# Attention with Fourier mixing on one core: storing every head pair's divided sums in 64-row transfers

## The chip, the core and the metric

The kernel runs on one core of a Trainium2 chip. The metric is the device time of one execution in microseconds (us). The kernel before takes 1719.1 us, the median of three runs (1718.28 to 1724.07). Its profiled execution took 1721.98 us.

## What is computed

The inputs are x (2048 rows, 512 columns), weights for an attention layer and matrices of a discrete Fourier transform. Cut to what matters:

```python
g = sigmoid((x * gate_w).sum(-1, keepdims=True))
q, k, v = split(x @ wqkv)                        # 32 heads of 16 columns
p = softmax(einsum("hqd,hkd->hqk", q, k) * 16 ** -0.5)
a = merge(einsum("hqk,hkd->hqd", p, v)) @ wo
b = dft_seq_re @ (x @ dft_hid_re.T) - dft_seq_im @ (x @ dft_hid_im.T)
return g * a + (1 - g) * b
```

## The kernel before

The program is one instruction stream per engine: TensorE (PE) multiplies, VectorE (DVE) and ScalarE (ACT) work on its results, GpSimd (POOL) does elementwise work and issues some transfers, and SyncE (SP) issues most of the others. The order on each engine is written out by hand: a schedule of steps, with loads, splits and stores placed at fixed step numbers.

Until about 665 us the kernel projects queries, keys and values, forms the first Fourier products, and scans many score blocks for row maxima, which the softmax needs before its exponentials. Then comes the main loop (L1197). It takes the 32 heads as 16 pairs, each pair as two halves of 1024 queries, and each half as 16 steps, one per block of 128 keys: 512 steps. The diff touches what is done with the result of each half, of which there are 32; the last is finished in another way behind the loop, so 31 go through the lines below.

One step does the following on PE: scores of a key block against 1024 queries (`qk`, L229), a scan block for a later pair's maxima (L154), and the sums of probabilities times values (`pv`, L775), which accumulate in one PSUM tile `pvb` over the 16 steps of a half. ACT forms the exponentials (L253, L261). DVE reduces each scan block to its maxima (L156); PE may not write the next scan block into that PSUM tile before DVE has read the last one. From step 317 on (MIX, at about 1268 us) the scans are over, and Fourier and output products (L204) take their place on PE.

`va`, the values, has a column of ones per head. So `pvb` holds, for each of four quarters (two heads and two blocks of 512 queries, at rows 0, 32, 64 and 96), 16 rows of sums and in a 17th row the softmax's denominators. When a half is complete:

- `quotients` (L782): DVE copies `pvb` into `ob` (L784). POOL issues four small transfers (L787) that spread the four rows of denominators over 128 partitions in `lc`.
- Ten steps later (L1240 to L1244), `divide` (L791): DVE takes the reciprocal of `lc` (L793). This instruction stands in DVE's stream among the reductions L156, so that one that waits here keeps the reductions behind it waiting. POOL then stores `lc` to DRAM (L794), loads it back as four broadcasts into `rb` (L796), multiplies (L797), rounds the product to `oh` (L808), takes the remainder `ol` (L811), and stores both to `o_d` (L803, or L806 for the last pair, which goes through SP's queue).

POOL issues its transfers in the order of its stream, and they travel on one queue, the profile's q0 (software_dynamic). SP's transfers are on q1 (hardware_dynamic). The next half's denominators (L787) come next on POOL's queue behind a half's two stores.

`o_d[f][i]` is a DRAM tile of shape 2, 2, 4, 64, 512: half, block of queries, pair within its group of four, 64 rows, 512 columns. One store of `oh` therefore writes two blocks of 64 rows by 2 KB that lie apart in DRAM, from 128 partitions in SBUF. These stores are read again only from 1562 us on, by SP's loads (L859, L867, L879, L882) for the output projection.

Of the kernel before, what the change touches and what calls it, by code (L numbers as in the profile page):

```python
# [10 lines left out]
F32 = mybir.dt.float32  # L11
# [12 lines left out]
NP = H // 2  # L24
# [42 lines left out]
def build(tc, xT, wqkv, wo, wrT, wiT, cr, ci, ct, gate, out):  # L67
    nc = tc.nc
    with ExitStack() as ctx:
# [18 lines left out]
        o_d = [[dram.tile([2, 2, NP // ND, 64, 512], F32, name=f"o_d{f}_{i}") for i in range(2)] for f in range(ND)]  # L88
# [181 lines left out]
        with ExitStack() as pf:  # L270
# [381 lines left out]
            with ExitStack() as py:  # L652
# [36 lines left out]
                for n, (ph, t, u) in enumerate(coef):  # L689
# [34 lines left out]
                    for w in range(CS):  # L724
                        s = u * CS + w
# [24 lines left out]
        with ExitStack() as pa:  # L750
# [40 lines left out]
            def divide(p, h, ob, lc):  # L791

                nc.vector.reciprocal(lc, lc)  # L793
                nc.gpsimd.dma_start(r_d[p][h].rearrange("n (s e) -> (n s) e", e=16), lc)  # L794
                for n, (c, j, r) in enumerate(quads):
                    nc.gpsimd.dma_start(rb[r:r + DH, :], r_d[p][h][n:n + 1, :].to_broadcast([DH, 512]))  # L796
                nc.gpsimd.tensor_mul(ob, ob, rb)  # L797
                oh, ol = (ap.tile([P, 512], F32R, tag=tag, name=tag) for tag in ("oh", "ol"))
                queue = nc.sync if p == NP - 1 else nc.gpsimd

                def store(i, s):
                    if p < NP - 1:
                        queue.dma_start(o_d[p // 4][i][h, :, p % 4], s.bitcast(F32))  # L803
                        return
                    for c in range(2):
                        queue.dma_start(o_d[p // 4][i][h, c, p % 4], s[64 * c:64 * c + 64, :].bitcast(F32))  # L806

                nc.gpsimd.tensor_copy(oh, ob)  # L808
                if p == NP - 1:
                    store(0, oh)  # L810
                nc.gpsimd.tensor_sub(ol, ob, oh.bitcast(F32))  # L811
                if p < NP - 1:
                    store(0, oh)
                store(1, ol)
# [382 lines left out]
            for step in range(NP * PERIODS):  # L1197
                p, i = step // PERIODS, step % PERIODS
                h, kb = i // NB, i % NB
# [132 lines left out]
```

## Time and profile before

| what | us |
|---|---|
| median of three runs | 1719.1 |
| profiled execution, its own time | 1721.98 |
| its span, from the first to the last instruction | 1720.2 |
| PE busy in the span | 1703.2 |
| ACT busy in the span | 1497.3 |
| DVE busy in the span | 1190.2 |
| POOL busy in the span | 752.1 |

How to read the profile: one execution, times in us from the span's start. A row of a view that groups instructions gives line, engine, operation, tiles (out<-in), shapes and count. A row of the timeline gives the start, the duration, and in brackets how long the engine had sat idle and what ended that. The view of waits gives who waited for whom: total, number of times, longest. The chain of waits is followed back from the last instruction. For a transfer issued by POOL the trace also has the time to landing; for one of SP it has not. The small difference between the execution's time and its span, 1.8 us, lies outside the instructions.

### The profile page before, as it was taken

What the parts mean: (1) busy time and instruction counts of PE and PEld (TensorE: products, weight loads), DVE (VectorE), ACT (ScalarE), POOL (GpSimd) and SP (SyncE); (2) the same over time, 40 slices, a digit from 0 to 9 for tenths busy, and PEclk for the clock granted to TensorE, in tenths of its full rate; (3) what the DMA queues carried; (4) which work ended last, traced back from release to release, by engine and by line L of the source; (5) the groups of instructions that cost most, each with busy time, mean ns of one, the idle gap of its engine ahead of it and who ended that gap; (6) DMA issues with size and microseconds to landing.
All of it is one profiled execution on the core that took longest, in us unless ns stands there. A gap on an engine that the chain in (4) does not pass through costs nothing.

```text
span 1720.2 us, 36368 instructions
## 1 busy us (share of the span) xinstructions
PE 1703.2 (99%) x13560; PEld 1029.4 (60%) x13560; DVE 1190.2 (69%) x2179; ACT 1497.3 (87%) x2472; POOL 752.1 (44%) x849
## 2 busy tenths in 40 slices
PE   9999999999999999999999999999999999999998
PEld 6888888989888795333333333333345555555554
DVE  6898888899999996666566666666742555654343
ACT  6447889888888888999899999999998888898876
POOL 3672435755555761434534445353422333334222
PEclk9999999999999999999999999999999999999999
DMA  7783457543337764456545545544445466676733
GB/s 254 242 287 77 149 160 215 161 112 107 107 112 199 181 127 95 93 116 157 109 111 140 121 114 114 120 112 97 76 93 135 130 150 146 148 150 167 194 104 126
DMA packets 174881, 241.17 MB, mean 140 GB/s; under 512 B 75968, under 2 KB 86704, under 8 KB 168112
## 3 DMA queue, kind: packets, MB, share of 16 engines
q1 hardware_dynamic: 133520, 217.27, 47.9%
q0 software_dynamic: 40608, 20.54, 6.1%
q8 instruction: 106, 1.74, 0.4%
q10 hardware_dynamic: 576, 1.05, 0.2%
q14 instruction: 71, 0.58, 0.1%
HBM read 158.34 MB, written 81.01 MB: 139 GB/s over the span
## 4 chain that ended last, share of the span: by engine, by line
PE 92%; DMA 4%; POOL 1%; DVE 1%; issue 1%; SPq 0%; ACT 0%; DVEq 0%; POOLq 0%
PE xy L204 26%; PE pvb L775 26%; PE s L229 17%; PE s L173 9%; PE s L204 9%; PE s L154 5%; DMA lc<-ob 2%; DMA rb<-r_d 1%; DMA r_d<-lc 1%; DMA raws<-wqkv 0%; POOL o_d L803 0%; POOL rb L796 0%; POOL lc L787 0%; POOL ob L797 0%; POOL ol L811 0%
## 5 line engine op out<-in xcount | busy, mean ns | idle before, releaser
L253 ACT ACTIVATE eb<-s 128x1024 f32<-128x1024 f32 x512 | 577.2, 1127 | 62.7 <-PE s L229 62.5
L261 ACT ACTIVATE e<-s 128x512 f32<-128x512 f32 x1022 | 606.5, 703 | 4.1 <-PE s L229 4.1
L156 DVE TENSOR_REDUCE mx<-s 128x2 f32<-128x1024 f32 x380 | 460.7, 1223 | 197.6 <-PE s L154 197.4
L775 PE MATMUL pvb<-eb,va 128*17 128x512 f32 x2052 | 516.1, 599 | 0.0
L775 PE MATMUL pvb<-e,va 128*17 128x512 f32 x2044 | 515.2, 599 | 0.0
L179 DVE CUSTOM_DVE_ANT_0 fold<-s,fold 128x512 f32<-128x512 f32 x644 | 433.5, 690 | 56.3 <-PE s L173 29.8
L177 ACT ACTIVATE fold<-s 128x512 f32<-128x512 f32 x644 | 381.6, 603 | 76.6 <-PE s L173 55.7
L229 PEld LDWEIGHTS s<-qs,ks 50*128 50x128 f32 x2048 | 212.9, 185 | 363.4 <-ACT eb L253 266.2
L229 PE MATMUL s<-qs,ks 50*128 50x512 f32 x2048 | 424.1, 436 | 0.0
L204 PE MATMUL xy<-b,c 64*128 64x512 f32 x2448 | 392.8, 392 | 0.3 <-ACT c L352 0.3
L173 PE MATMUL s<-ks,qs 48*128 48x512 f32 x1288 | 304.1, 403 | 1.3 <-DVE mx L179 0.9
L204 PEld LDWEIGHTS xy<-b,c 64*128 64x128 f32 x2448 | 282.8, 187 | 18.9 <-issue 1.0
L173 PEld LDWEIGHTS s<-ks,qs 48*128 48x128 f32 x1288 | 165.6, 184 | 40.6 <-DVE mx L179 10.2
L775 PEld LDWEIGHTS pvb<-eb,va 128*17 128x17 f32 x2052 | 69.8, 96 | 190.5 <-issue 181.2
L154 PE MATMUL s<-ks,qs 48*128 48x512 f32 x760 | 158.6, 396 | 4.8 <-DVE mx L156 4.6
L204 PE MATMUL s<-b,b 64*128 64x512 f32 x1050 | 136.7, 391 | 0.0
L794 POOL DMA_DIRECT2D r_d<-lc x31 | 18.3, 591 | 223.5 <-DVE lc L793 197.2
L204 PE MATMUL xy<-w,b 64*128 64x512 f32 x768 | 114.9, 392 | 0.0
L204 PEld LDWEIGHTS s<-b,b 64*128 64x128 f32 x1050 | 100.2, 185 | 23.8 <-issue 1.0
L384 POOL TENSOR_TENSOR c<-craw,c 128x512 fp32r<-128x512 f32 x84 | 110.4, 1314 | 6.7
L787 POOL DMA_DIRECT2D lc<-ob x124 | 64.4, 526 | 110.9 <-DVE ob L784 110.7
L967 POOL TENSOR_TENSOR sum<-craw 128x512 f32<-128x512 f32 x60 | 75.5, 1286 | 79.0 <-DMA kept_None<-sum 57.6
(148 smaller groups left out, 1538.9 us busy)
## 6 DMA issues: line engine op xcount, KB each, us to landing
qs<-q_d SPq DMA_DIRECT2D x68, 256.0 KB
craw<-cr SPq DMA_DIRECT2D x60, 256.0 KB
craw<-ct SPq DMA_DIRECT2D x48, 256.0 KB
ks<-k_d SPq DMA_DIRECT2D x46, 256.0 KB
kept_None<-sum SPq DMA_DIRECT2D x40, 256.0 KB
craw<-kept_None SPq DMA_DIRECT2D x40, 256.0 KB
qs<-q_d SPq DMA_DIRECT2D x68, 128.0 KB
craw<-ci SPq DMA_DIRECT2D x32, 256.0 KB
```

The source lines that it names most:

```text
L154: nc.tensor.matmul(ps[:, j, :], qs[b:b + 48, qb * P:(qb + 1) * P], ks[b:b + 48, c * 512:(c + 1) * 512], start=True, stop=True)
L156: nc.vector.tensor_reduce(mx[p][:, :, qb, c], ps, axis=AX.X, op=ALU.max)
L173: nc.tensor.matmul(ps, qs[b:b + 48, qb * P:(qb + 1) * P], ks[b:b + 48, c * 512:(c + 1) * 512], start=True, stop=True)
L177: nc.scalar.activation(fold[j], ps, AF.Relu)
L179: nc.vector.tensor_tensor_reduce(out=fold[j], in0=ps, in1=fold[j], scale=1.0, scalar=-3.0e38, op0=ALU.add, op1=ALU.max, accum_out=mx[p][:, ...
L204: nc.tensor.matmul(ps[j], lhs[r], rhs[r], start=first, stop=last)
L229: nc.tensor.matmul(pss[j], ks[b:b + 50, kb * P:(kb + 1) * P], qs[b:b + 50, q0:q0 + 512], start=True, stop=True)
L253: nc.scalar.activation(e, ps, AF.Exp, scale=SCALE)
L261: nc.scalar.activation(e[j], pss[j], AF.Exp, scale=SCALE)
L384: sub(lo, raw, hi.bitcast(F32))
L775: nc.tensor.matmul(pvb[r:r + VC, :], va[:, kb, 2 * p + j, :], es[c][j], start=kb == 0, stop=kb == NB - 1, tile_position=(0, r))
L967: (nc.gpsimd.tensor_add if terms[1][1] > 0 else nc.gpsimd.tensor_sub)(s, *(raws[k] for k, sign in terms))
```

## The change

For the pairs 0 to 14, the store of `oh` and that of `ol` become two transfers each, of 64 rows by 512 columns, in place of one that names two blocks of 64 rows. The last pair's stores have had this form already. The queue is as before: POOL's for the pairs 0 to 14, SP's for pair 15. The stores go to the same places and hold the same values. On POOL a half thus issues 13 transfers in place of 11; no other engine's instructions change, nor their order. Lines behind L801 move up by three.

```diff
@@ -799,9 +799,6 @@
                 queue = nc.sync if p == NP - 1 else nc.gpsimd
 
                 def store(i, s):
-                    if p < NP - 1:
-                        queue.dma_start(o_d[p // 4][i][h, :, p % 4], s.bitcast(F32))
-                        return
                     for c in range(2):
                         queue.dma_start(o_d[p // 4][i][h, c, p % 4], s[64 * c:64 * c + 64, :].bitcast(F32))
```

## The prediction

> **What bounds the kernel now.** The page comes first: which engine is full, and how much room the one that issues the changed transfers has.
>
> ```profile
> span 1720.2 us, 36368 instructions
> ...
> PE 1703.2 (99%) x13560; PEld 1029.4 (60%) x13560; DVE 1190.2 (69%) x2179; ACT 1497.3 (87%) x2472; POOL 752.1 (44%) x849
> ```
>
> PE is busy 99% of the span, so only what lets PE wait or slows it can count; POOL, at 44%, has slack on average. Where does PE lose anything in the main loop? The view of waits says that, first by PE alone, then for the engine that PE waited for.
>
> ```profile
> PE s L154 <- DVE mx L156: 4.6, 2, 3.4
> ...
> DVE lc L793 <- DMA lc<-ob: 8.4, 4, 4.3
> ```
>
> PE waits 4.6 us for DVE's reductions, in two places, and DVE in turn waits 8.4 us, four times, for the denominators' transfer `lc`. The chain of waits, cut to a window around the longest, tells what came before:
>
> ```profile
> 806.77 13.39 DMA rb<-r_d
> ...
> 823.62 1.65 POOL o_d L803 x2
> ...
> 826.79 9.12 DMA lc<-ob
> 836.04 0.25 DVE lc L793
> 836.29 1.09 DVE mx L156
> 837.42 0.79 PE s L154 x2
> ```
>
> Read it upwards. PE's scan block of 837.42 waited for a reduction, that one for the reciprocal, that one for `lc`, which landed 9.12 us after its issue, right behind two stores of `o_d` on POOL's queue. POOL was late because `rb` had taken 13.39 us. The store's own cost to PE is thus one of waiting, and the timeline of PE shows its size. These are scan blocks, one per step:
>
> ```profile
> 831.98 0.40 PE L154 MATMUL s<-ks,qs 48*128 48x512 f32 x2
> ...
> 837.42 0.79 PE L154 MATMUL s<-ks,qs 48*128 48x512 f32 x2 [3.39 <-DVE mx L156]
> ...
> 841.00 0.63 PE L154 MATMUL s<-ks,qs 48*128 48x512 f32 x2
> ...
> 844.31 0.40 PE L154 MATMUL s<-ks,qs 48*128 48x512 f32 x2
> ...
> 846.20 0.40 PE L154 MATMUL s<-ks,qs 48*128 48x512 f32 x2
> ```
>
> An undisturbed step takes 846.20 - 844.31 = 1.89 us. From 831.98 to 844.31 there are three, which took 12.33 in place of 5.67: **6.66 us lost**. Of that 3.39 is idle time. The rest is slowness: the same pair of matmuls takes 0.79 and 0.63 us before it is back at 0.40. The table by stage shows it in the granted clock (the number ahead of the last two):
>
> ```profile
> 700.00:800.00 100.00, 100.00 (x740) 38.15 (x734) 67.75 (x63) 100.00 (x160) 40.89 (x53) 1.00 0.49 113
> 800.00:900.00 100.00, 96.61 (x694) 35.84 (x695) 63.75 (x61) 93.90 (x149) 39.35 (x52) 0.97 0.59 122
> ```
>
> The stage with the stall has a mean clock of 0.97, its neighbour 1.00. Two more places lose time:
>
> ```profile
> 959.79 0.39 PE L154 MATMUL s<-ks,qs 48*128 48x512 f32 x2
> ...
> 963.95 0.40 PE L154 MATMUL s<-ks,qs 48*128 48x512 f32 x2
> ```
>
> ```profile
> 1081.34 0.39 PE L154 MATMUL s<-ks,qs 48*128 48x512 f32 x2
> ...
> 1084.58 0.50 PE L154 MATMUL s<-ks,qs 48*128 48x512 f32 x2 [1.19 <-DVE mx L156]
> ...
> 1086.58 0.40 PE L154 MATMUL s<-ks,qs 48*128 48x512 f32 x2
> ```
>
> Each stretch is two steps, 3.78 us. They took 4.16 and 5.24: 0.38 and 1.46 lost. DVE's fourth wait made no wait of PE, which has two entries above. In all 6.66 + 0.38 + 1.46 = **8.50 us**: the most that the change can give back through `lc`.
>
> **The change part by part.**
>
> *Landing.* What do the stores take, and what does a 64-row store take? First their time to landing, in the last column of the issues; then the extremes over all 60 of them, in the view of line 803; then the packets in a window that holds two stores of one half and almost nothing else.
>
> ```profile
> o_d<-oh POOLq DMA_DIRECT2D x30, 256.0 KB, 11.3
> o_d<-ol POOLq DMA_DIRECT2D x30, 256.0 KB, 12.6
> ```
>
> ```profile
> DMA to landing us min/median/max: 8.5/12.0/19.2
> ```
>
> ```profile
> DMA packets 1090, 0.59 MB, mean 51 GB/s; under 512 B 944, under 2 KB 944, under 8 KB 1088
> ...
> q0 software_dynamic: 1056, 0.53, 19.4%
> q1 hardware_dynamic: 32, 0.03, 0.9%
> ```
>
> The window is 1657.5 to 1669. A median store lands after 11.3 or 12.6 us, and the fastest of all after 8.5. In the window the bytes are 0.53 MB, the two stores, but 944 of 1090 packets are tiny and 144 carry data. Of the two stores' share, q1's 32 halved between data and marks, 128 carry data, 64 for each store; 0.53 MB over 128 is 4 KB each. That leaves some 928 tiny ones, 464 per store: 16 for the 16 engines' completion, and 448, which is 14 times 32, where 64 is 2 times 32. I read this as two of sixteen engines carrying 32 data packets each and fourteen going through 32 fillers each. It is a reading of counts, not a row that says so. The address that the store is given has 2 as its first count (2, 64, 512), and the new one has 64.
>
> For 64 rows the nearest row is that of the last pair, the same shape on SP's queue:
>
> ```profile
> 1683.02 1.40 SPq L806 DMA_DIRECT2D o_d<-oh  x2
> 1684.52 1.19 SPq L806 DMA_DIRECT2D o_d<-ol  x2
> 1685.82 2.48 SPq L879 DMA_DIRECT2D b<-o_d  x4
> ...
> L879 SPq EVENT_SEMAPHORE  x4: 17/22/28, 1685.8 to 1687.7; - x4
> ```
>
> The loads L879 read what was just stored, one after the other, and their waits took 17 to 28 ns, so the first store, issued at 1683.02, had landed by 1685.82: at most 2.8 us. That is another queue, and an upper end there. The other end is 11.3 us, no better than now. I take 2.8, because the shape is the changed one and POOL's transfers with 16 or more rows first land as fast when nothing is ahead of them, as the minimum below shows.
>
> The Trainium skill speaks on both sides here. "DMA: Bandwidth & Descriptors", section "Why a DMA increments its semaphore by 16 and not by 1", says that the number of engines is the largest up to 16 that divides the first count other than 1 on both sides: two for the old store, 16 for the new. The packet counts above agree with the two; no run here yet shows the 16. Against the change, the same page's section "Rules for kernel authors" says of two transfers to halves of the partitions "Don't bother — they serialize" and advises one transfer of 128. By the first rule the sum is as below, by the second it would be zero at best, the first rival.
>
> *Issue on POOL.* Two more transfers per half, 60 in all. By form, the durations on POOL:
>
> ```profile
> L787 POOL DMA_DIRECT2D lc<-ob x124 | 64.4, 526 | 110.9 <-DVE ob L784 110.7 <-issue 0.2
> ...
> L803 POOL DMA_DIRECT2D o_d<-oh x30 | 26.4, 879 | 0.0
> L803 POOL DMA_DIRECT2D o_d<-ol x30 | 24.8, 827 | 0.0
> ...
> L794 POOL DMA_DIRECT2D r_d<-lc x31 | 18.3, 591 | 223.5 <-DVE lc L793 197.2 <-DVE b L1008 26.3
> ```
>
> Two stores take 0.879 + 0.827 = 1.71 us. A 64-row issue is not in POOL's rows. Its lower bound is half of today's, 0.42, which adds nothing; its upper is today's price of a whole one, 0.879, so that four take 3.52 and add 1.81. I take 0.56, between the 0.526 of 32 rows and the 0.591 of 128 rows without the leading 2: four are 2.24, and 0.53 us is added per half, 16 us of POOL in all. POOL waits 197 us in L794's row alone for DVE's reciprocal, which hides it, unless POOL is late, as in the chain above.
>
> *The sum at the stall.* The reciprocal was due when DVE had done its reduction:
>
> ```profile
> 830.52 1.23 DVE L156 TENSOR_REDUCE mx<-s 128x2 f32<-128x1024 f32 x1 [0.66 <-PE s L154]
> ```
>
> ```profile
> DMA to landing us min/median/max: 1.5/9.7/16.9
> ```
>
> That is 831.75. (The second row is of `lc`, each of the 124 transfers.) The stores begin at 823.6 as before, since `rb` was issued ahead of them and has none of them in front of it. Four issues end at 825.9, four of `lc` at 0.526 at 828.0. The last, issued at 827.4, lands at 828.9 by the minimum of 1.5 us and at 830.2 by the 2.8 of a 64-row store: 1.5 to 2.8 us early. With 1.81 in place of 0.53 on POOL it would be 831.5, still 0.2 early. At the two other places DVE waited less:
>
> ```profile
> 960.58 0.25 DVE L793 RECIPROCAL lc<-lc 128x16 f32<-128x16 f32 x1 [1.03 <-DMA lc<-ob]
> ```
>
> ```profile
> 1083.19 0.25 DVE L793 RECIPROCAL lc<-lc 128x16 f32<-128x16 f32 x1 [2.08 <-DMA lc<-ob]
> ```
>
> From the median of 9.7 us to 2.8, `lc` gains 6.9, less 0.53 on POOL: more than these 1.03 and 2.08, and more than the longest, 4.3. So **all 8.50 us go**.
>
> What is late next? PE itself. DVE's rows elsewhere wait for PE, ACT's share is 87%, and SP waits for nothing that POOL stores until 1562 us. There SP's loads of the stored sums find them sooner; PE's waits at the end are not for them. The stores' bytes are the same, on more engines for a shorter time; SP's transfers lose at most what they gain where they met the two slow ones.
>
> 1720.2 - 8.5 = 1711.7 for the span, and the 1.78 us by which the profiled execution exceeds its span make **1713.5 us**. Against that execution this is 0.49%; against the median of 1719.1, 0.33%. The three runs spread over 5.8 us. That is the size of these stalls with and without the slow clock (8.50, or 3.39 + 0.38 + 1.46 = 5.2), so 1718.3 would be a run without it, with the same floor. The page of one execution can't prove that.
>
> **The rivals.**
>
> *The transfers are no faster*: landing depends on the queue's contention and not on the shape, so the change cuts the stores and brings nothing earlier. For it: the longest of 19.2 us is over twice the shortest, and SP's traffic is what differs between them. Against it: even the fastest store took 8.5 us, and in the quiet window there was next to no other traffic. PE's stalls stay, 1719 to 1722 us. The Trainium skill's rule against splitting, in the second section named above, comes to the same.
>
> *Part of it:* `lc` comes 1 to 2 us late at the longest place, below what slowed the clock; the others go. 1713.5 + 1.5 = 1715.
>
> *Slower:* landing stays as it is and POOL pays 0.879 per issue. Where POOL is late, `lc` then goes out 1.81 us later, and PE's three stalls each grow by that: 3 x 1.81 = 5.4. Should the one at 1081 to 1086 reach the length at which the first lost its clock (1.19 idle of its own and 1.81 are near 3.39), 6.66 - 3.39 = 3.3 more. 1722.0 + 5.4 = 1727.4, up to 1730.7. It decides where the four issues cost more than the stores' landing saves; by the sum above that point is not reached at all if landing falls below 3 us.
>
> **How the numbers follow.** Chances: the forecast 0.74, no faster 0.10, part 0.06, slower 0.10. A measurement of this kernel can tell about 0.3% from no change, 5.2 us, so faster means below 1713.9. The forecast lies just below that; if runs without the profiler have smaller stalls than the profiled one, the gain from the median is smaller. I give two thirds of the forecast's chance to faster, 0.49, the rest with the two middle cases to the same, 0.41, and 0.10 to slower. Range: low, if an undisturbed run loses all 8.5 us from the median, 1710.6, and 1 us of spread below it, 1709.5; high 1720.0, which takes in part and most of the unchanged case.
>
> **What would show it.** In the profile after: landing of `o_d` near 3 us and not 11; `lc` at 1.5 to 3 at the median in place of 9.7; no tiny fillers in a quiet window; no wait of DVE L793 for `lc`; clock 1.00 in 800 to 900; four issues per half on POOL near 0.56 each; a span near 1711.7. Wrong would be: stores landing as late as now, a wait of L793 that stays, issues near 0.88, or PE waits at a place that now has none.

## The result and the profile after

The changed kernel takes 1714.38 us, the median of 7 runs (1713.46 to 1717.08); the kernel before, over 7 runs, 1723.2 (1718.28 to 1724.66). The ratio is **0.9958**, with a 95% interval of 0.9944 to 0.9972: 0.42% faster. The forecast was 1713.5. The profiled execution of the changed kernel took 1715.43 us, with a span of 1713.6.

The waits of PE from 660 us on are the first thing to look at. This is the whole list for the changed kernel:

```profile
PE s L1277 <- DVE rb L1274: 0.9, 1, 0.9
```

The two waits of L154 for DVE's reductions, 4.6 us, are gone; what is left lies behind the main loop and was there before. DVE itself waits for `lc` once, not four times:

```profile
DVE lc L793 <- DMA lc<-ob: 1.8, 1, 1.8
```

The table by stage has the clock back at 1.00 and PE full where it had been at 0.97 and 96.61:

```profile
800.00:900.00 100.00, 100.00 (x742) 38.32 (x734) 67.86 (x64) 100.00 (x160) 42.32 (x59) 1.00 0.56 127
```

Why: the stores' landing, in the last column of the issues, and that of `lc` in the view of its line (minimum, median, maximum):

```profile
o_d<-oh POOLq DMA_DIRECT2D x60, 128.0 KB, 3.0
o_d<-ol POOLq DMA_DIRECT2D x60, 128.0 KB, 3.6
```

```profile
DMA to landing us min/median/max: 1.5/3.2/10.1
```

11.3 and 12.6 became 3.0 and 3.6, and `lc` came down from 9.7 to 3.2 at the median. POOL at the place of the old stall, in the timeline:

```profile
817.21 1.95 POOL L796 DMA_DIRECT2D rb<-r_d  x4 [13.47 <-DMA r_d<-lc]
...
824.09 1.13 POOL L803 DMA_DIRECT2D o_d<-oh  x2
825.21 1.05 POOL L803 DMA_DIRECT2D o_d<-ol  x2
826.26 1.96 POOL L787 DMA_DIRECT2D lc<-ob  x4
```

POOL is as late as before: it lost 13.47 us waiting for `r_d`, where it had been `rb` before, and `lc` goes out at 826.3 (825.3 before). But nothing slow is ahead of it now, and DVE, when it gets to the reciprocal, doesn't wait (no bracket):

```profile
832.98 0.24 DVE L793 RECIPROCAL lc<-lc 128x16 f32<-128x16 f32 x1
```

### The profile page after: what moved, and what is told of

It reads as the page before. It is cut to its first block, busy times and chain, and to the rows that moved or that the text cites. A ratio compares the mean times of both kernels' runs of the same rounds, so it can differ in the third digit from the quotient of the medians.

```text
span 1713.6 us, 36496 instructions
## 1 busy us (share of the span) xinstructions
PE 1700.1 (99%) x13560; PEld 1033.2 (60%) x13560; DVE 1189.9 (69%) x2179; ACT 1496.6 (87%) x2472; POOL 764.1 (45%) x909
## 3 DMA queue, kind: packets, MB, share of 16 engines
q0 software_dynamic: 14688, 20.33, 5.0%
## 4 chain that ended last, share of the span: by engine, by line
PE 95%; issue 1%; POOL 1%; DMA 1%; DVE 1%; ACT 0%; SPq 0%; DVEq 0%; POOLq 0%; ACTq 0%
PE pvb L775 29%; PE xy L204 24%; PE s L229 19%; PE s L173 9%; PE s L204 9%; PE s L154 5%; POOL el L297 1%; DMA raws<-wqkv 0%; DMA qs<-q_d 0%; DVE y L890 0%; DVE fold L179 0%; ACT fold L177 0%; DVE s L297 0%; SPq L543 0%; SPq L542 0%
## 5 line engine op out<-in xcount | busy, mean ns | idle before, releaser
L154 PE MATMUL s<-ks,qs 48*128 48x512 f32 x760 | 158.5, 394 | 0.9 <-DMA qs<-q_d 0.9
L796 POOL DMA_DIRECT2D rb<-r_d x124 | 60.5, 494 | 110.6 <-DMA r_d<-lc 104.7
```

The source lines that it names most:

```text
L154: nc.tensor.matmul(ps[:, j, :], qs[b:b + 48, qb * P:(qb + 1) * P], ks[b:b + 48, c * 512:(c + 1) * 512], start=True, stop=True)
```

## The experiments

My theory: a store whose first count is 2 runs on two engines and lands late; `lc` comes behind it on POOL's queue; DVE waits for `lc`, and PE for DVE. The rivals: any smaller transfer would land earlier; or the slow stores hurt in another way, by holding up SP's transfers; or POOL's issues are what counts. All ratios are to the kernel before in the same comparison; several kernels share one.

**One transfer, 128 as the first count.** The DRAM tile puts both blocks of a pair side by side; SP's loads at the end are split in two for it.

```diff
-dram.tile([2, 2, NP // ND, 64, 512], ...)
+dram.tile([2, NP // ND, 2, 64, 512], ...)
-queue.dma_start(o_d[p // 4][i][h, :, p % 4], s.bitcast(F32))
+queue.dma_start(o_d[p // 4][i][h, p % 4].rearrange("c r s -> (c r) s"), s.bitcast(F32))
```

> The store stays one transfer of 256 KB per tile, but the DRAM tile is laid out so that its 128 rows are one even run: the first count is 128, not 2. The price is on the reading side: each of SP's loads of the stored sums from 1562 us on becomes two. If the first count decides (engines count): landing of the stores near 3 to 4 us instead of 11.3 and 12.6, lc near 3 us at the median, no wait of PE for DVE in the main loop, no half clock, time 1713 to 1716, that is 0.995 to 0.997 of before, the same as the changed kernel within 0.2%. If the size of one transfer decides: landing stays at 9 to 12 us, DVE waits for lc four times as before, ratio 0.999 to 1.001. POOL issues two stores at about 0.6 us each, less than the 1.71 of before and the 2.18 of after.

Ratio 0.9982 (0.9968 to 0.9996), median 1716.16.

```profile
o_d<-oh POOLq DMA_DIRECT2D x30, 256.0 KB, 2.4
o_d<-ol POOLq DMA_DIRECT2D x30, 256.0 KB, 3.5
```

The same 256 KB in one transfer land in 2.4 and 3.5 us: the size was not it, the form of the address was. The edit changes two things in that form at once. The first count is 128 and no longer 2, and the 128 rows are one even run in DRAM and no longer two runs that lie apart. No run here has a large first count and a broken run, so times alone can't tell the two apart; the packets below speak for the count.

PE's waits in the main loop are gone here too. The time was expected to be that of the changed kernel, 1713 to 1716, and is 2.2 us above it (1713.95 beside it on the same chip, below). PE's waits have a new row:

```profile
PE s L204 <- DMA b<-o_d: 1.4, 2, 0.8
```

That is the price at the end: near 1683 us PE waits twice for the doubled loads. The two profiled executions differ by 2.2 us as well. The last copy of the loop (L784) comes at 1662.7 here and at 1662.2 in the changed kernel beside it, so 1.7 of the 2.2 us lie behind the main loop, and these waits are 1.4 of them.

**Halved by columns, first count still 2.**

```diff
-queue.dma_start(o_d[p // 4][i][h, :, p % 4], s.bitcast(F32))
+for q in (slice(0, 256), slice(256, 512)):
+    queue.dma_start(o_d[p // 4][i][h, :, p % 4, :, q], s[:, q].bitcast(F32))
```

> The stores are halved as in the changed kernel, to 128 KB each and four per half, but by columns: 2 x 64 x 256, so the first count stays 2. If the first count decides: each transfer still goes to two engines, landing of a store stays above 5 us, the tiny packets on POOL's queue grow rather than vanish, POOL pays about 0.83 per issue (3.3 us per half in place of 1.7), lc at the median stays above 6 us and at least two of the four waits of DVE for lc stay; ratio 0.998 to 1.004. If the size of one transfer decides: as the changed kernel, landing near 3 us, ratio 0.995 to 0.997.

Ratio **1.0045** (1.0024 to 1.0067), median 1727.73: four transfers of 128 KB, as in the changed kernel, and slower than before, just above the range expected. They land after 7.2 and 8.4 us, and PE waits at three places:

```profile
PE s L154 <- DVE mx L156: 6.8, 3, 2.8
```

`lc` at the median is at 5.9, a hair under the 6 expected, since part of its wait has moved to POOL, which was not expected; DVE waits for it five times, 12.6 us. The timeline of POOL at the old stall:

```profile
821.63 1.71 POOL L804 DMA_DIRECT2D o_d<-oh  x2
823.32 0.80 POOL L804 DMA_DIRECT2D o_d<-ol  x1
827.95 0.80 POOL L804 DMA_DIRECT2D o_d<-ol  x1 [3.83 <-issue]
828.74 2.03 POOL L787 DMA_DIRECT2D lc<-ob  x4
```

Ahead of the fourth store POOL stands still for 3.83 us, waiting for nothing that the profile shows; over all 30 halves this comes to 140.3 us. This kernel is the rival of the other side, POOL held up while the stores still land late, and it is slower as that rival said.

**The old stores, behind `lc` instead of ahead.** For the pairs 0 to 13 a half's two stores are kept back until the next half's `lc` has been issued.

```diff
+while held:            # at the end of quotients, behind the four transfers of lc
+    held.pop(0)()
...
+if p < NP - 2:
+    held.extend([lambda: store(0, oh), lambda: store(1, ol)])
+    return
```

> The stores keep the old form, 2 x 64 x 512 and slow, but for the pairs 0 to 13 POOL issues them behind the next half's four lc transfers instead of ahead of them. If what cost time was lc queued behind slow stores: the stores still land after 9 to 19 us, but lc lands 1 to 4 us after its issue at the median, no wait of PE for DVE, ratio 0.995 to 0.997 as in the changed kernel. If the slow stores cost time in another way (they hold up SP's transfers, or their own landing is waited for): the gain is missing, ratio 0.999 to 1.001. A new wait could be that of r_d and of the next cast to oh behind the stores.

Ratio 0.9959 (0.9944 to 0.9975), median 1714.52. The stores are as slow as ever and the time is that of the changed kernel:

```profile
o_d<-oh POOLq DMA_DIRECT2D x30, 256.0 KB, 10.6
o_d<-ol POOLq DMA_DIRECT2D x30, 256.0 KB, 11.4
rb<-r_d POOLq DMA_DIRECT2D x124, 32.0 KB, 2.2
lc<-ob POOLq DMA_DIRECT2D x124, 2.0 KB, 2.6
```

So slow stores cost no time in themselves that this comparison can tell; only `lc` behind them did. That takes the rival of SP's transfers away. `r_d` lands at 4.0 us here, 2.6 before, and POOL bears it.

**The changed kernel again,** on the chip of these three.

> The changed kernel once more, on the chip of the other three, so that they can be compared with it: ratio to before 0.994 to 0.997, landing of the stores 3.0 and 3.6 us, four issues on POOL in 2.18 us per half, no PE wait for DVE in the main loop.

Ratio 0.9965 (0.9952 to 0.9977), median 1713.95 of 12 runs (1713.43 to 1714.99), span 1711.7. The stores land after 2.6 and 3.7 us, and PE does not wait for DVE in the main loop.

**A third store ahead of `lc`, first try.** In the kernel before, `ol` is stored twice.

```diff
 if p < NP - 1:
     store(0, oh)
+    store(1, ol)
 store(1, ol)
```

> The kernel before with the store of ol issued twice for the pairs 0 to 14 (the same bytes to the same place, so the result is unchanged): three slow stores ahead of each lc in place of two. If the slow stores ahead of lc are what costs: lc lands some 3 to 6 us later where POOL is late (near 834, 960, 1083 us) and in other halves whose slack was under 1 us, DVE waits for lc in at least 8 halves in place of 4, PE waits for DVE over 12 us in total, the clock falls to half more than once, and the time is 1735 to 1790. If the stores' number ahead of lc does not matter: four waits and 1718 to 1726. POOL may also be held at an issue, as it was with four such stores.

A single run took 1906.29 us, far above what was expected, and not for the reason I meant to test:

```profile
POOL o_d L803 <- DMA o_d<-ol: 398.4, 30, 19.9
```

The second store goes to the place of the first, so the program makes it wait until that one has landed: 398.4 us over 30 halves. The edit added a wait, and this kernel tells nothing of a third store that is only queued. What it does show is what happens to PE when `lc` is late in 26 halves: PE waits 112.9 us for DVE's reductions and has a mean clock of 0.951.

**A third store, second try,** into a spare DRAM tile; and, in the changed kernel, the same bytes as two more 64-row transfers.

```diff
+queue.dma_start(spare[p][h][:, 0], oh.bitcast(F32))                              # kernel before
+for c in range(2):                                                               # changed kernel
+    queue.dma_start(spare[p][h][c, 0], oh[64 * c:64 * c + 64, :].bitcast(F32))
```

> The kernel before with a third slow store ahead of lc, now without a dependency: oh is stored once more, as 2 x 64 x 512, into a spare DRAM tile that nothing reads (pairs 0 to 14). If slow stores ahead of lc are what costs, a third one lands lc 3 to 6 us later: DVE waits for lc in 8 or more halves, PE waits for DVE over 12 us in total, half clock in more than one place, time 1735 to 1800, ratio 1.01 to 1.05. POOL may be held at the third issue as it was at the fourth of the store by columns. If only the two stores of the design matter, or SP's traffic alone decides, ratio 0.998 to 1.004.

> The changed kernel with the same extra 256 KB per half, but as two 64-row transfers into the spare tile: six 64-row transfers ahead of lc. If it is the form and not the bytes that makes lc late: each lands near 3 to 4 us, POOL spends 1.1 us more per half, lc lands 1 to 2 us later where POOL is late, which is within what DVE leaves (3.7 us at the fourth half), PE does not wait for DVE or below 1 us, ratio 0.994 to 0.998. If the bytes count, ratio above 1.0.

The slow one: ratio **1.008** (1.0055 to 1.0104), median 1734.78, just below the range expected. `lc` lands after 12.9 us at the median, DVE waits in 9 halves, and:

```profile
PE s L155 <- DVE mx L157: 12.8, 3, 6.1
```

POOL was not held at the third issue. The fast one: ratio 0.9958 (0.994 to 0.9977), median 1714.46, `lc` at 3.4 us, no wait of PE for DVE in the loop. The same 256 KB more per half cost over 13 us in one form and nothing in the other.

**Cut once more, to 32 rows.**

```diff
-queue.dma_start(o_d[...][h, c, p % 4], s[64 * c:64 * c + 64, :].bitcast(F32))
+for r in (0, 32):
+    queue.dma_start(o_d[...][h, c, p % 4, r:r + 32], s[64 * c + r:64 * c + r + 32, :].bitcast(F32))
```

> The changed kernel with each 64-row store cut once more, to 32 rows by 512: eight issues per half for the pairs 0 to 14, first count 32. If the count of engines decides and POOL's issue time is hidden: each issue takes 0.50 to 0.55 us, 4.1 to 4.4 us per half instead of 2.18, landing stays near 3 us, lc goes out 2 us later where POOL is late and still lands 1 to 2 us before DVE needs it, no PE wait or one below 1 us, ratio to before 0.994 to 0.998, as the changed kernel. If issue time on POOL counts: the waits at 834, 960 and 1083 come back, ratio 0.998 to 1.003.

Ratio 0.9965 (0.9951 to 0.9978), median 1715.52. Eight issues of 0.50 to 0.52 us,

```profile
L805 POOL DMA_DIRECT2D o_d<-oh x120 | 61.2, 516 | 0.0
L805 POOL DMA_DIRECT2D o_d<-ol x120 | 59.0, 498 | 0.1
```

4.1 us per half on POOL in place of 2.2, landing after 2.9 and 4.7 us, and no wait of PE in the loop: issue time on POOL is hidden at this size.

**Only `oh` in 64 rows.**

> Half of the change: oh is stored in two 64-row transfers, ol in one of 2 x 64 x 512 as before. If the slow store ahead of lc is what costs, one of them is enough to keep lc late, but less: landing of oh 3 to 4 us, of ol 6 to 12, lc at the median 4 to 8 us (3.2 with all of the change, 9.7 with none), one or two waits of DVE for lc left where POOL is late, PE's longest wait below 3 us and no half clock, ratio 0.995 to 0.999. If any first 64-row store were enough, it would equal the changed kernel, lc near 3 us.

(The edit: the old branch is kept for `i == 1`.) Ratio 0.9974 (0.9955 to 0.9993), median 1716.84. PE's longest wait is 2.6 us, with no half clock, as expected. The loop, from the first copy of `pvb` to the last (L784), takes 975.3 us against 971.4 in the changed kernel: the 3.9 us are PE's two waits, 4.0 us, and nothing is lost to slow instructions behind them. `lc` was not where I had put it (4 to 8 us), and DVE waits for it four times, 8.3 us, not once or twice:

```profile
lc<-ob POOLq DMA_DIRECT2D x124, 2.0 KB, 8.9
```

One slow store left keeps `lc` nearly as late (8.9 of 9.7) as two. The landing of `lc` is not shared out by bytes among what is ahead; one slow store is enough.

**What the packets say of the two engines.** The count of packets on POOL's queue in the whole execution can be worked out. A slow store had 64 data packets, 448 fillers and 16 marks, 528 in all, by my reading. Before, 60 of these leave 40608 - 31680 = 8928 for everything else. A transfer that uses all engines should have its data and 16 marks: 32 + 16 = 48 with 128 KB.

| kernel | worked out | 
|---|---|
| changed | 8928 + 120 x 48 = 14688 |
| 128 as first count | 8928 + 60 x (64 + 16) = 13728 |
| columns, 7 fillers per data packet | 8928 + 120 x (32 + 224 + 16) = 41568 |
| third slow store | 8928 + 90 x 528 = 56448 |

The rows of the four kernels, in that order:

```profile
q0 software_dynamic: 14688, 20.33, 5.0%
```

```profile
q0 software_dynamic: 13728, 20.32, 4.2%
```

```profile
q0 software_dynamic: 41568, 20.76, 6.0%
```

```profile
q0 software_dynamic: 56448, 28.51, 7.8%
```

Each agrees to the packet, and so do the other three with 8928 and the same parts: 16608 with 32 rows, 27648 with only `oh` in 64 rows, 17568 with the fast spare stores. Fillers come with a first count of 2, seven for each data packet, fourteen to two, and with no other form tried. Their share is the same where the run in DRAM is broken once (before) and where it is broken behind every row (by columns), which speaks for the count and not for the break. That two engines carry the data is still an inference from these counts, since the trace names no engine; but nothing here speaks against it.

## Why the prediction was right, point by point

- **The bound and the mechanism** held: late stores, late `lc`, DVE's reciprocal, the reduction, PE. The old stores behind `lc` show the queue's order as the link, the third store shows its size, and one transfer of 128 rows, with the packets, points to the first count as the cause of the late landing.
- **Landing**: put at 2.8 from SP's queue; 3.0 and 3.6 measured. The lower and upper ends, 2.8 and 11.3, were far apart, and the row of the same shape was the one to trust. `lc` was put at 1.5 to 2.8; its median is 3.2, with a maximum of 10.1. The four `lc` issued from 1306.7 us on landed after 8.7 to 9.5 us, though the last store ahead of them had gone out by 1298.7. The DMA engines were full there (the share ahead of the last number; it is 1.00 to 1.06 from 1300 to 1320):

```profile
1305.00:1310.00 5.00, 5.00 (x46) 2.39 (x38) 2.75 (x5) 4.52 (x8) 2.18 (x4) 1.00 1.05 201
```

  I had taken the transfers' own form as all that matters for landing; here a late landing stands beside full engines with no slow store in sight. That the traffic made it late is argued from this row, not tested.
- **Issue on POOL**: 0.56 us assumed. The rows of the changed kernel:

```profile
L803 POOL DMA_DIRECT2D o_d<-oh x60 | 34.0, 569 | 0.0
L803 POOL DMA_DIRECT2D o_d<-ol x60 | 31.7, 532 | 0.7 <-issue 0.7
```

  34.0 + 31.7 = 65.7 us over 120 is 0.55; the upper bound of 0.879 was far off.
- **The sum**: 8.50 us were to go. From the first copy of `pvb` to the last of the loop (L784) it was 691.4 to 1670.6 before and is now

```profile
L784 DVE COPY ob<-pvb x31: 691/692/694, 692.7 to 1664.1; 128x512 f32<-128x512 f32 x31
```

  979.2 less 971.4: **7.8 us** gained in the loop of the profiled execution. No more was there to gain: the loop takes 971.3 to 971.5 us in all five kernels in which PE does not wait for DVE in it. The step that was sized too high is the loss at the three places. Set each reduction of the kernel before beside the same one of the changed kernel's second profiled execution, and the delay grows by what was lost. At the longest place it is 0.57 us ahead of the stall (830.52 less 829.95) and 7.02 when the pace is steady again:

```profile
869.22 1.23 DVE L156 TENSOR_REDUCE mx<-s 128x2 f32<-128x1024 f32 x1 [0.51 <-PE s L154]
```

```profile
862.20 1.23 DVE L156 TENSOR_REDUCE mx<-s 128x2 f32<-128x1024 f32 x1 [0.51 <-PE s L154]
```

  That is 6.45 us, and by the same count the two other places cost 0.21 and 1.25: 7.9 in all, where the prediction had 6.66, 0.38 and 1.46. It counted up to the first quick scan block, and a part of the delay is made up in the steps behind it (7.22 us at 844.75, 7.02 at 869.22).

  Ahead of the loop, where no changed instruction has run, the executions differ too: the first copy comes at 692.7 here, at 691.4 before and at 690.8 in the second profiled execution. That is why the spans of the two are 1713.6 and 1711.7. So it is luck that the second has just the span that was forecast: 7.8 us of its gain come from the loop and 0.6 from ahead of it.
- **What would be late next**: PE, as said. Near 834 us the chain of waits is now PE's alone. One thing was wrong: I expected no wait of DVE for `lc`. One of 1.8 us is left, for the `lc` of 1306.7 above, where PE has no scan block to wait with. It is the fourth wait of the kernel before (0.99 us, ended at 1324.6), so one of the four comes without slow stores too.
- **The rule against splitting**: "DMA: Bandwidth & Descriptors", section "Rules for kernel authors", of the Trainium skill would have had halves bring nothing. Here the two halves landed in 3.0 to 3.6 us and the one transfer in 11.3 to 12.6, so the measurement differs from it for a transfer whose first count is 2. With 128 as the first count one transfer is as fast, 2.4 to 3.5, which agrees both with that section's advice to use one transfer of 128 partitions and with the Trainium skill's rule on the first count, in the other section of that page that the prediction names.
- **The rivals**: "no faster" fell with the landing; "slower" came true in the store by columns, where the landing stayed slow and POOL paid more, at 1.0045. "Part of it" did not come: at the longest place `lc` was in time.
- **The median**: I read the spread of the three runs as stalls with and without the slow clock, and a floor of 1713.5. Later runs of the kernel before spread further: the lowest of 32 in the second comparison was 1715.34. So the stalls vary more from run to run than two states, and that reading was too neat. The changed kernel's spread there is 1.6 us over 12 runs. The kernel before has a median of 1723.2 over seven runs and not the 1719.1 of three, so the 0.42% beside a forecast of 0.33% is in part the chance of which runs came first. The line drawn for faster, 1713.9, was missed by half a microsecond (1714.38), and the largest single chance, 0.49, had been put below it.

No version beats the changed kernel. The old stores behind `lc` equal it (0.9959 beside 0.9965, with intervals that overlap), and PE has no wait left in the main loop to take.

## What to carry to other kernels

A transfer that nobody waits for can cost time through what is queued behind it: look at what lands late and ask what stood ahead of it on its queue, not only at who waits for the slow one. Write the address of a transfer so that its first count is large, 64 or 128 and not 2; one even run of 128 rows lands as early as two transfers of 64. When a stall of an engine is followed by slow instructions, price it by the time until the old pace is back: here 3.39 us of idle time cost 6.45.

## What the runs showed of the hardware that I had not expected

The clock does not follow the length of a gap alone. In the store by columns PE was idle for 1.85 us at 834 and for 2.14 us at 1085. After the shorter one the scan blocks were slow, after the longer one not:

```profile
835.84 0.50 PE L154 MATMUL s<-ks,qs 48*128 48x512 f32 x2 [1.85 <-DVE mx L156]
...
838.58 0.63 PE L154 MATMUL s<-ks,qs 48*128 48x512 f32 x2
```

```profile
1086.69 0.50 PE L154 MATMUL s<-ks,qs 48*128 48x512 f32 x2 [2.14 <-DVE mx L156]
...
1088.68 0.39 PE L154 MATMUL s<-ks,qs 48*128 48x512 f32 x2
```

0.63 against 0.39 for the same pair of matmuls, and the mean granted clock is 0.98 in the stage from 800 to 900 us and 1.00 in that from 1000 to 1100. A forecast for a stall of 2 us has thus to hold both prices. And POOL can stand still at an issue for a reason that no row names: with four stores in a row whose first count is 2 (128 KB each) it did so at the fourth in each of 30 halves, with three of 256 KB or eight with a first count of 32 it did not. What it waited for stays open. The changed kernel has such rows too, one of 5.72 us ahead of a load of `rb` at 1143 us, without a wait of PE for DVE.
